# Packing the last 64 channels of two rows into one transpose in a fused dynamic-convolution and gated-FFN kernel

## The chip, the cores and the metric

The kernel runs on one core of a Trainium2 chip. The metric is the device time of one execution in microseconds (us), given as the median of three runs, with the lowest and highest beside it. The profile is one further execution of the same program, recorded by the hardware profiler; its span is counted from the first to the last instruction.

## The reference

Two stages in float32. First a dynamic convolution: for each of 4 x 4160 positions and 8 heads, seven softmax weights mix the current row of `x` (192 channels, 24 to a head) with the six rows before it. Then a gated feed-forward layer of width 1024, with a convolution of three taps over the positions inside the gate.

```python
w = exp(weight_gen - max); w = w / (sum(w) + 1e-9)          # [B, S, 8, 7]
y[b, s, h, :] = sum over k of w[b, s, h, k] * x_pad[b, s + k, h, :]
h = maximum(y @ w_in, 0)                                    # [B, S, 1024]
conv[s] = sum over k in 0..2 of conv_w[k] * h_pad[s + k]
out = (h * sigmoid(conv)) @ w_out                           # [B, S, 192]
```

## The kernel before, in words

The 16640 positions are dealt out as 130 consecutive rows to each of 128 partitions. They are worked through in 33 blocks `q` of R = 4 rows (512 positions).

**Taps and folds.** For each block, seven products of a row window with a weight (`tap`, L292) are written by GpSimd (POOL) or VectorE (DVE) into two tiles: `px` with four slots of 128 x (4 rows x 192 channels), and `py` with three. In blocks 0 to 2 TensorE (PE) adds the seven products itself, while it transposes them, in PSUM. In the other 30 blocks the sum is made before that: an accumulating DMA adds `py` onto `px[0:3]` (`fold1`, L315), a second one adds `px[2:4]` onto `px[0:2]` (`fold2`, L318), and one POOL addition of 768 elements per partition adds slot 1 onto slot 0 (`fold3`, L322). `px` has three buffers; taps of a later block wait until the transposes have read the old one.

**Transposes.** The folded block has positions on its partitions and must have channels there. `transposes` (L327) does this on PE in two parts through one PSUM bank, `tp`. Part 0 takes channels 0 to 127 of each of the four rows: four transposes, each with a loaded operand of 128 columns. Part 1 takes channels 128 to 191: four transposes with a loaded operand of 64 columns. Every transpose streams the 128 columns of an identity. After each part the PSUM bank is read by two engines: ScalarE (ACT) copies it into a rounded high part (`split_hi`, L338), then DVE subtracts that from the bank and writes the low part (`split_lo`, L343). Part 1 gives the tile `H2`, with the high part in partitions 0 to 63 and the low part in 64 to 127. Part 1 may overwrite the bank only after the subtraction of part 0.

**Feed-forward.** For each of eight groups `f` of 128 hidden channels, `mm1` (L359) runs five matmuls of 512 columns into one of five PSUM banks `z`; then follow `relu` and `wmid` on ACT, two side taps on DVE (L376), a tanh on ACT (L383) and the gate product on DVE (L392), which frees the bank. Two blocks later `mm2` (L405) runs four output tiles of eight accumulating matmuls, each of 192 columns.

**Order.** Every instruction is a task with an engine and an assumed duration. A planner, at the end of the function, places all tasks from those durations, once forward, once backward and once forward again, and the instructions are issued in the order of the planned starts. Each engine then runs its own list in that order and waits on semaphores.

Of the kernel before, what the change touches and what calls it, by code (L numbers as in the profile page):

```python
# [8 lines left out]
F32 = mybir.dt.float32  # L9
# [3 lines left out]
ACTF = mybir.ActivationFunctionType  # L13
ALU = mybir.AluOpType
AX = mybir.AxisListType

P = 128
# [34 lines left out]
def vec(n, ps=1):  # L52

    return 0.07 + n / 960 + 0.06 * ps


def act(n, ptr=0):
    return 0.05 + n / 1200 + 0.1 * ptr


def pool(n, ins=2):
    return (0.13 + n / 437) if ins == 2 else (0.1 + n / 900)
# [3 lines left out]
def kernel(  # L66
# [9 lines left out]
    nc = tc.nc  # L76
    B, S, D = x.shape
# [5 lines left out]
    D2 = D - P  # L83
# [7 lines left out]
    R = 4  # L91
# [18 lines left out]
    ident = const.tile([P, P], F32, name="ident")  # L110
# [73 lines left out]
    def group(q):  # L184
        return (q + 1) // 2
# [95 lines left out]
    def tap_cut(q, k):  # L281
        return max(0, slot(R * q - TAPS + k) + R - RING) % R
# [17 lines left out]
    px_t, py_t, h_t = {}, {}, {}  # L300

    def piece(q, i):
        if i < 4:
            if q not in px_t:
                px_t[q] = px_p.tile([P, 4, R, D], F32, tag="px", name="px")
            return px_t[q][:, i]
        if q not in py_t:
            py_t[q] = py_p.tile([P, 3, R, D], F32, tag="py", name="py")
        return py_t[q][:, i - 4]
# [4 lines left out]
    def fold1(q):  # L314
        nc.gpsimd.dma_start(out=fl4(px_t[q][:, 0:3]), in_=fl4(py_t[q][:, 0:3]), accum_op=ALU.add, max_dma_last_dim=3072)  # L315

    def fold2(q):
        nc.gpsimd.dma_start(out=fl4(px_t[q][:, 0:2]), in_=fl4(px_t[q][:, 2:4]), accum_op=ALU.add, max_dma_last_dim=3072)  # L318

    def fold3(q):  # L320
        a, b = (px_t[q][:, i].rearrange("p s d -> p (s d)") for i in range(2))
        nc.gpsimd.tensor_tensor(out=a, in0=a, in1=b, op=ALU.add)  # L322

    def transposes(q, i, part, dst, start, stop):
        src = piece(q, i)
        for c in range(R):
            nc.tensor.matmul(  # L327
                dst[0:D2 if part else P, c * P:(c + 1) * P],
                lhsT=src[:, c, part * P:part * D2 + P],
                rhs=ident, is_transpose=True, start=(start and c == 0), stop=(stop and c == R - 1),  # L330
            )

    def split_hi(q, part, tp):
        if (q, "H1") not in h_t:
            for nm in ("H1", "L1", "H2"):
                h_t[q, nm] = t_p.tile([P, W], F32R, tag=nm, name=nm)
        r = slice(0, D2 if part else P)
        nc.scalar.activation(out=h_t[q, "H2" if part else "H1"][r, :], in_=tp[r, :], func=ACTF.Copy)  # L338

    def split_lo(q, part, tp):  # L340
        H = h_t[q, "H2" if part else "H1"]
        r = slice(0, D2 if part else P)
        nc.vector.tensor_tensor(  # L343
            out=H[D2:P, :] if part else h_t[q, "L1"], in0=tp[r, :], in1=H[r, :].bitcast(F32), op=ALU.subtract
        )

    z_t, g_t = {}, {}

# [73 lines left out]
    V, G = nc.vector, nc.gpsimd  # L422

    with tc.manual_schedule():
# [7 lines left out]
        def load_in(eng, kind, a, b):  # L432
# [17 lines left out]
            out=ident, in_=ident, pattern=[[-1, P]], base=0, channel_multiplier=1,  # L450
# [4 lines left out]
            out=edge, in_=edge, pattern=[[1, TAPS], [1, TAPS]], base=-TAPS, channel_multiplier=0,  # L455
# [31 lines left out]
        def task(eng, dur, deps, fn=None, after=(), begun=()):  # L487
            edges = [(d, dur_of(d) + lat(d, eng)) for d in deps if d is not None]
            edges += [(d, dur_of(d)) for d in after if d is not None]
            edges += [(d, 0.0) for d in begun if d is not None]  # L490
            tasks.append((eng, dur, edges, fn))
            prio.append(now[0])
            return len(tasks) - 1

        def dur_of(d):
            return tasks[d][1]

        ENDS = {"V": 0.125, "A": 0.14, "G": 0.08, "P": 0.2, "D": 0.0, "H": 0.0, "none": 0.05}

        def lat(d, eng):  # L500
            e = tasks[d][0]
            if e == eng == "P":
                return 0.02
            return ENDS[e[0] if e != "none" else e] + {"P": 0.02, "G": 0.045}.get(eng, 0.0)

        def dma(occ, deps, fn):
            return task("none", 3.2, [task("H", occ, deps, fn)])

# [73 lines left out]
        for c, (kind, a, b, t, eng, wle) in enumerate(CH):  # L582
# [7 lines left out]
            if kind == "m":  # L590
                hi, lo = wh[:, 0, a:b], wl[:, 0, a:b]
            else:
                th = tB.bitcast(F32R).rearrange("p (l f) -> p l f", l=2)
                hi, lo = th[:, 0, 0:n], th[:, 1, 0:n]
            a_ = task("A", act(n) + 0.02, [j_], lambda bits=bits, hi=hi: nc.scalar.activation(  # L595
                out=hi, in_=bits().bitcast(F32), func=ACTF.Copy))
            if pm:
                wle = "V"
            b_ = task("V" if pm else "VK" if wle == "V" else "G", vec(n, pm) if wle == "V" else pool(n), [a_],
                      lambda bits=bits, hi=hi, lo=lo, wle=wle: (V if wle == "V" else G).tensor_tensor(  # L600
                out=lo, in0=bits().bitcast(F32), in1=hi.bitcast(F32), op=ALU.subtract))
# [7 lines left out]
            else:  # L609
# [10 lines left out]
                b_ = dma(2.6, [b_], spread)  # L620
# [19 lines left out]
        bank = {0: [c2], 1: [], 2: dbank[0]}  # L640
        NU = NB * NF

        def dadd(deps, occ, fn, e):
            return task("none", 3.2, [task("D", occ, [task("G", e, deps, fn)])])
# [9 lines left out]
        def head(q):  # L654
            how, engs = PLAN[q] if q < len(PLAN) else REST
            prod = {}
            xdep, ydep = xf_[-NX:][:1] if q >= NX else [], yf_[-NY:][:1] if q >= NY else []
            for i, k in ((0, 0), (1, 1), (2, 2), (4, 4), (5, 5), (6, 6), (3, 3)):
                e = engs[i]
                E_, d_ = (V, vec(R * D, 0)) if e == "V" else (G, 1.5)  # L660
                d_ += 0.14 * (tap_cut(q, k) > 0)
                p_ = task("VK" if e == "V" else e, d_, [sm[group(q)], x_t_[q]] + (xdep if i < 4 else ydep),
                          lambda E_=E_, k=k, i=i: tap(E_, q, k, piece(q, i)), begun=[gp[0]] if e == "G" else [])
                if e == "G":
                    gp[0] = p_
                prod[i] = p_
                all_taps.setdefault(q, []).append(p_)
            if how == "a":
                out_ = [(i, prod[i]) for i in (0, 1, 2, 4, 5, 6, 3)]
            else:  # L670
                a_ = dadd([prod[i] for i in (0, 1, 2, 4, 5, 6)], 6.5, lambda: fold1(q), 0.82)
                yf_.append(a_)
                out_ = [(3, prod[3]), (0, a_), (1, a_), (2, a_)]
                if how != "b":
                    a_ = dadd([a_, prod[3]], 4.4, lambda: fold2(q), 0.775)
                    out_ = [(0, a_), (1, a_)]
                    if how != "c":
                        out_ = [(0, task("G", 1.78, [a_], lambda: fold3(q)))]
            multi = len(out_) > 1
            now[0] = q + FO  # L680
            hold, prev = {}, [None, None]
            hd = [mm_end[q - 2]] if q >= 2 else []
            xend, yend = [], []
            for n, (i, e_) in enumerate(out_):
                first, last = n == 0, n == len(out_) - 1
                for part in (0, 1):
                    b_ = part if multi else 0

                    def fold(i=i, part=part, b_=b_, first=first, last=last):
                        if first:  # L690
                            hold[part] = (ps_o if b_ else ps_t).tile(
                                [P, W], F32, tag="ops" if b_ else "tp", name="ops" if b_ else "tp")
                        transposes(q, i, part, hold[part], first, last)
                    f_ = task("P", 0.46, [e_] + (bank[b_] if first else [prev[part]]), fold)
                    prev[part] = f_
                    (xend if i < 4 else yend).append(f_)
                    if last:
                        a_ = task("A", 0.49, [f_] + hd, lambda part=part: split_hi(q, part, hold[part]))
                        l_ = task("V", 0.6, [a_], lambda part=part: split_lo(q, part, hold[part]))
                        spl_done.setdefault(q, []).append(l_)  # L700
                        bank[b_] = [l_]
            xf_.append(task("none", 0.0, xend))
            if yend:
                yf_.append(task("none", 0.0, yend))
# [54 lines left out]
        def attention(q):  # L759
            now[0] = q + TO  # L760
            loads(q)
            head(q)
# [145 lines left out]
```

## Time and profile before

| | |
|---|---|
| median of 3 runs | 713.72 us (713.22 to 714.27) |
| the profiled execution's own time | 713.11 us |
| its span | 711.4 us |
| PE busy in the span | 690.1 us, 97% |
| PE weight loads (PEld) | 629.0 us, 88% |
| DVE busy | 625.6 us, 88% |
| ACT busy | 549.9 us, 77% |
| POOL busy | 510.5 us, 72% |

Busy shares are averages over the whole span, and matmuls overlap in the pipeline, so the length of one matmul's record is more than the time by which it delays the next. The chain that ended last follows the work back from the final instruction and gives each step only the time by which it delayed the end. In the page's 40 slices the granted clock of PE is at its top level (the digit 9, 2.4 GHz) throughout.

### The profile page before, as it was taken

The page shows a single profiled execution, that of the slowest core. Times are in us where ns is not written, and L with a number is a line of the kernel's source. Part 1 is how long each engine was busy: PE and PEld are TensorE (multiplying, and loading weights), DVE is VectorE, ACT ScalarE, POOL GpSimd, SP SyncE. Part 2 cuts the span into 40 slices and gives each one's busy share as a digit, 9 for nine tenths or more (in the row PEclk, how much of TensorE's full clock was granted, in tenths as well). Part 3 has the DMA queues.
Part 4 walks back from the last instruction along what each step waited for, and adds up shares of the span by engine and source line. Part 5 has one row for each costly group of instructions (what it writes and reads, how often), then busy time and mean ns, then how long its engine had stood idle before and what let it go on. Part 6 is the DMA issues. An engine that isn't in the chain of part 4 may idle for free.

```text
span 711.4 us, 10938 instructions
## 1 busy us (share of the span) xinstructions
PE 690.1 (97%) x3809; PEld 629.0 (88%) x3809; DVE 625.6 (88%) x975; ACT 549.9 (77%) x1049; POOL 510.5 (72%) x392
## 2 busy tenths in 40 slices
PE   1899999999999999999999999999999999999998
PEld 1788999999999999999999999999999999999998
DVE  6999998989999998998898988988898888888981
ACT  2588888887888787878787877878778778787881
POOL 3998999999987778887777778877767788630000
PEclk9999999999999999999999999999999999999999
DMA  7736999898989688798888788788879886781211
GB/s 226 212 98 166 215 217 225 211 236 197 229 186 211 166 208 200 167 209 189 193 193 200 190 181 202 184 200 193 188 181 200 178 183 163 163 181 68 76 43 45
DMA packets 70787, 127.59 MB, mean 179 GB/s; under 512 B 5046, under 2 KB 42573, under 8 KB 70732
## 3 DMA queue, kind: packets, MB, share of 16 engines
q0 software_dynamic: 20160, 58.99, 46.9%
q1 hardware_dynamic: 50090, 67.51, 29.3%
q8 instruction: 30, 0.49, 0.3%
q10 hardware_dynamic: 482, 0.40, 0.2%
q14 instruction: 25, 0.20, 0.1%
HBM read 20.51 MB, written 12.78 MB: 47 GB/s over the span
## 4 chain that ended last, share of the span: by engine, by line
PE 96%; DMA 2%; DVE 1%; POOL 0%; SPq 0%; ACT 0%; issue 0%; POOLq 0%
PE ops L405 47%; PE z L359 43%; PE tp L327 5%; DMA ring<-in_x_dram 1%; PE ops L327 1%; PE z L405 1%; DMA stage<-in_moe_w_in_dram 1%; DVE py L292 0%; POOL px L292 0%; POOL py L292 0%; SPq L437 0%; DVE r L257 0%; DVE m L248 0%; DVE w L242 0%; DVE px L292 0%
## 5 line engine op out<-in xcount | busy, mean ns | idle before, releaser
L376 DVE SCALAR_TENSOR_TENSOR z<-h,cw,z 128x512 f32<-128x512 f32 (+1 forms) x528 | 379.3, 741 | 25.7 <-ACT z L369 21.3
L405 PE MATMUL ops<-wo,g 128*128 128x192 f32 x2048 | 353.1, 326 | 0.0
L405 PEld LDWEIGHTS ops<-wo,g 128*128 128x128 f32 x2048 | 338.9, 190 | 10.0
L359 PE MATMUL z<-H,wi 128*128 128x512 f32 x1056 | 303.6, 409 | 1.0 <-ACT wi L595 1.0
L292 POOL TENSOR_TENSOR px<-ring,w 128x768 f32<-128x768 f32 (+2 forms) x146 | 231.9, 1702 | 79.6 <-PE tp L327 75.3
L359 PEld LDWEIGHTS z<-H,wi 128*128 128x128 f32 x1056 | 191.1, 189 | 32.5 <-ACT wi L595 1.4
L392 DVE SCALAR_TENSOR_TENSOR g<-z,h 128x512 f32<-128x512 f32 (+1 forms) x264 | 178.3, 679 | 22.3 <-ACT z L383 14.6
L383 ACT ACTIVATE z<-z 128x512 f32<-128x512 f32 (+1 forms) x264 | 151.3, 573 | 45.2 <-DVE z L376 43.4
L369 ACT ACTIVATE z<-h,cw 128x512 f32<-128x512 f32 (+1 forms) x264 | 179.9, 682 | 5.7
L365 ACT ACTIVATE h<-z 128x512 f32<-128x512 f32 x264 | 155.7, 590 | 29.1 <-PE z L359 27.8
L292 POOL TENSOR_TENSOR py<-ring,w 128x768 f32<-128x768 f32 (+2 forms) x108 | 162.8, 1813 | 2.2 <-DMA px<-py 2.2
L359 PE MATMUL z<-L,wi 128*128 128x512 f32 x264 | 103.1, 391 | 0.0
L322 POOL TENSOR_TENSOR px<-px 128x768 f32<-128x768 f32 x30 | 68.0, 2265 | 6.1 <-DMA px<-px 6.1
L414 ACT ACTIVATE o<-ops 128x192 f32<-128x192 f32 x128 | 41.9, 328 | 24.0 <-PE ops L405 22.8
L359 PEld LDWEIGHTS z<-L,wi 128*128 128x128 f32 x264 | 49.6, 188 | 11.2
L338 ACT ACTIVATE H<-tp 128x512 fp32r<-128x512 f32 (+1 forms) x63 | 37.3, 593 | 21.5 <-PE tp L327 20.1
L327 PE MATMUL tp<-ident,px 128*128 128x128 f32 (+1 forms) x288 | 44.5, 279 | 2.7 <-POOL px L292 1.9
L315 POOL DMA_DIRECT2D px<-py x30 | 41.3, 1377 | 7.2 <-POOL py L292 7.2
L318 POOL DMA_DIRECT2D px<-px x30 | 36.3, 1211 | 13.2 <-DMA px<-py 12.0
L327 PEld LDWEIGHTS tp<-ident,px 128*128 128x128 f32 (+1 forms) x288 | 34.6, 132 | 9.5 <-POOL px L292 2.4
L343 DVE TENSOR_TENSOR L<-tp,H 128x512 fp32r<-128x512 f32 x33 | 22.7, 687 | 6.9 <-ACT H L338 6.9
L343 DVE TENSOR_TENSOR H<-tp,H 64x512 fp32r<-64x512 f32 x30 | 20.5, 684 | 6.7 <-ACT H L338 5.9
(67 smaller groups left out, 180.4 us busy)
## 6 DMA issues: line engine op xcount, KB each, us to landing
px<-py POOLq DMA_DIRECT2D x30, 1152.0 KB, 10.2
h<-h SPq DMA_DIRECT2D x128, 256.0 KB, 4.4
px<-px POOLq DMA_DIRECT2D x30, 768.0 KB, 6.6
ring<-in_x_dram SPq DMA_DIRECT2D x31, 384.0 KB, 6.0
out_dram<-o SPq DMA_DIRECT2D x31, 384.0 KB, 2.4
w<-in_weight_gen_dram SPq DMA_DIRECT2D x15, 224.0 KB, 6.5
r_out<-in_moe_w_out_dram SPq DMA_DIRECT2D x4, 384.0 KB, 5.6
wi<-scr SPq DMA_DIRECT2D x8, 128.0 KB, 5.2
```

The source lines that it names most:

```text
L292: eng.tensor_tensor(out=dst[:, a:b, :].rearrange("p s (h g) -> p s h g", g=GRP), in0=ring[:, p:p + n, :].rearrange("p s (h g) -> p s h g", ...
L322: nc.gpsimd.tensor_tensor(out=a, in0=a, in1=b, op=ALU.add)
L327: nc.tensor.matmul(dst[0:D2 if part else P, c * P:(c + 1) * P], lhsT=src[:, c, part * P:part * D2 + P], rhs=ident, is_transpose=True, star ...
L343: nc.vector.tensor_tensor(out=H[D2:P, :] if part else h_t[q, "L1"], in0=tp[r, :], in1=H[r, :].bitcast(F32), op=ALU.subtract)
L359: nc.tensor.matmul(out=z, lhsT=w[:, fs], rhs=h_t[j, nm], start=(i == 0), stop=(i == len(terms) - 1))
L365: nc.scalar.activation(out=hrow(f, 2, R), in_=z_t[j, f], func=ACTF.Relu)
L369: nc.scalar.activation(out=z_t[j, f][:, :no * P], in_=hrow(f, cc, no), func=ACTF.Copy, scale=cw[:, NF + f:NF + f + 1])
L376: nc.vector.scalar_tensor_tensor(out=z, in0=hrow(f, cc + d, no), scalar=cw[:, k * NF + f:k * NF + f + 1], in1=z, op0=ALU.mult, op1=ALU.add,)
L383: nc.scalar.activation(out=z, in_=z, func=ACTF.Tanh, scale=0.5)
L392: nc.vector.scalar_tensor_tensor(out=g_of(j, f), in0=z_t[j, f][:, :no * P], scalar=1.0, in1=hrow(f, cc, no), op0=ALU.add, op1=ALU.mult)
L405: nc.tensor.matmul(out=ps[:, 0:D], lhsT=g_of(j, f)[:, i * P:(i + 1) * P], rhs=wo[:, f, :], start=(f == 0), stop=(f == NF - 1),)
L414: nc.scalar.activation(out=o_t[j][:, i, :], in_=ps[:, 0:D], func=ACTF.Copy, scale=0.5)
```

## The change

`fold3` becomes two POOL instructions instead of one. Both read slots 0 and 1 of `px` and write slot 2 (instead of slot 0) in another layout: first the first 128 channels of the four rows, 4 x 128 elements, then the last 64 channels of the four rows side by side, 4 x 64 elements. So in part 1 two rows fill one loaded operand of 128 columns, and part 1 takes two transposes instead of four; their result lies in all 128 partitions of 256 columns of the bank. As one of the two rows comes out in partitions 64 to 127, the split of part 1 runs as two instructions of 64 x 256 on ACT and two on DVE, one for each row of the pair. The numbers of the planner's tasks are changed with it. Blocks 0 to 2 (`i >= 0`) are as before.

```diff
     def fold3(q):
-        a, b = (px_t[q][:, i].rearrange("p s d -> p (s d)") for i in range(2))
-        nc.gpsimd.tensor_tensor(out=a, in0=a, in1=b, op=ALU.add)
+        c = px_t[q][:, 2].rearrange("p s d -> p (s d)")
+        a, b = px_t[q][:, 0], px_t[q][:, 1]
+        for lo, hi, dst in ((0, P, c[:, 0:R * P]), (P, D, c[:, R * P:])):
+            nc.gpsimd.tensor_tensor(
+                out=dst.rearrange("p (s d) -> p s d", s=R), in0=a[:, :, lo:hi], in1=b[:, :, lo:hi], op=ALU.add
+            )
+    R2 = R // 2
     def transposes(q, i, part, dst, start, stop):
-        src = piece(q, i)
-        for c in range(R):
+        if i < 0:
+            src = px_t[q][:, 2].rearrange("p s d -> p (s d)")
+            ops = [(dst[:, c * P:(c + 1) * P], src[:, (part * R + c) * P:(part * R + c + 1) * P])
+                   for c in range(R2 if part else R)]
+        else:
+            src = piece(q, i)
+            ops = [(dst[0:D2 if part else P, c * P:(c + 1) * P], src[:, c, part * P:part * D2 + P]) for c in range(R)]
+        for c, (o, a) in enumerate(ops):
             nc.tensor.matmul(
...
+    def parts(q, part, tp, pairs):
+        H = h_t[q, "H2" if part else "H1"]
+        if not part:
+            return [(tp, H, h_t[q, "L1"])]
+        if not pairs:
+            return [(tp[0:D2], H[0:D2], H[D2:P])]
+        rows = H.rearrange("p (a b t) -> p a b t", a=R2, b=2)
+        return [(tp[b * D2:(b + 1) * D2, 0:R2 * P].rearrange("p (a t) -> p a t", a=R2), rows[0:D2, :, b], rows[D2:P, :, b])
+                for b in range(2)]
...
+        for src, hi, lo in parts(q, part, tp, pairs):
+            nc.scalar.activation(out=hi, in_=src, func=ACTF.Copy)
+    def split_lo(q, part, tp, pairs):
+        for src, hi, lo in parts(q, part, tp, pairs):
+            nc.vector.tensor_tensor(out=lo, in0=src, in1=hi.bitcast(F32), op=ALU.subtract)
...
-                        out_ = [(0, task("G", 1.78, [a_], lambda: fold3(q)))]
+                        out_ = [(-1, task("G", 2.02, [a_], lambda: fold3(q)))]
...
-                    f_ = task("P", 0.46, [e_] + (bank[b_] if first else [prev[part]]), fold)
+                    pr = i < 0 and part == 1
+                    f_ = task("P", 0.24 if pr else 0.46, [e_] + (bank[b_] if first else [prev[part]]), fold)
...
-                        a_ = task("A", 0.49, [f_] + hd, lambda part=part: split_hi(q, part, hold[part]))
-                        l_ = task("V", 0.6, [a_], lambda part=part: split_lo(q, part, hold[part]))
+                        a_ = task("A", 0.56 if pr else 0.49, [f_] + hd, lambda part=part, pr=pr: split_hi(q, part, hold[part], pr))
+                        l_ = task("V", 0.78 if pr else 0.6, [a_], lambda part=part, pr=pr: split_lo(q, part, hold[part], pr))
```

## Rows read from the trace of the kernel before

**Rows 1.** The page: busy time of each engine, then the chain by engine.
```profile
PE 690.1 (97%) x3809; PEld 629.0 (88%) x3809; DVE 625.6 (88%) x975; ACT 549.9 (77%) x1049; POOL 510.5 (72%) x392
...
PE 96%; DMA 2%; DVE 1%; POOL 0%; SPq 0%; ACT 0%; issue 0%; POOLq 0%
```

**Rows 2.** All waits of PE: who for whom, us in total, times, longest.
```profile
PE tp L567 <- DVE tok L874: 14.4, 1, 14.4
PE tp L327 <- POOL px L292: 1.9, 2, 1.3
PE z L359 <- ACT wi L595: 1.0, 1, 1.0
PE tp L327 <- DVE px L292: 0.8, 1, 0.8
```

**Rows 3.** Busy time by stretch: the stretch, its length, each engine, clock, DMA.
```profile
75.00:697.00 622.00, 622.00 (x3412) 568.96 (x3411) 559.26 (x837) 499.02 (x940) 452.27 (x337) 1.00 0.80 183
```

**Rows 4.** The chain that ended last, 300 to 345 us: start, us, what.
```profile
303.33 0.44 PE tp L327 x4
...
319.58 0.44 PE tp L327 x4
320.02 1.16 PE z L359 x5
```

**Rows 5.** Transposes by shape: count, us busy, mean ns of one, idle before.
```profile
L327 PE MATMUL tp<-ident,px 128*128 128x128 f32 x168 | 26.5, 284 | 2.7 <-POOL px L292 1.9 <-DVE px L292 0.8
...
L327 PEld LDWEIGHTS tp<-ident,px 128*128 128x128 f32 x168 | 21.4, 147 | 7.9 <-POOL px L292 2.4 <-DVE px L292 1.2 <-issue 0.3
...
L327 PE MATMUL tp<-ident,px 128*64 128x128 f32 x120 | 18.0, 273 | 0.0
...
L327 PEld LDWEIGHTS tp<-ident,px 128*64 128x64 f32 x120 | 13.2, 112 | 1.5
```

**Rows 6.** The same view: copies and subtractions from PSUM, 512 and 256 columns.
```profile
L343 DVE TENSOR_TENSOR H<-tp,H 64x512 fp32r<-64x512 f32 x30 | 20.5, 684 | 6.7 <-ACT H L338 5.9
...
L338 ACT ACTIVATE H<-tp 64x512 fp32r<-64x512 f32 x30 | 17.7, 590 | 1.3
...
L600 DVE TENSOR_TENSOR wi<-dps,wi 128x256 fp32r<-128x256 f32 x2 | 0.8, 424 | 0.0
...
L595 ACT ACTIVATE wi<-dps 128x256 fp32r<-128x256 f32 x2 | 0.8, 383 | 3.8 <-DVE dps L151 3.8
```

**Rows 7.** The same view: POOL, the last fold and taps of several sizes.
```profile
L292 POOL TENSOR_TENSOR px<-ring,w 128x768 f32<-128x768 f32 x116 | 204.5, 1850 | 67.1 <-PE tp L327 62.8 <-DMA px<-py 4.1
...
L322 POOL TENSOR_TENSOR px<-px 128x768 f32<-128x768 f32 x30 | 68.0, 2265 | 6.1 <-DMA px<-px 6.1
...
L292 POOL TENSOR_TENSOR px<-ring,w 128x384 f32<-128x384 f32 x10 | 9.3, 1031 | 12.5 <-PE tp L327 12.5
...
L292 POOL TENSOR_TENSOR px<-ring,w 128x192 f32<-128x192 f32 x10 | 8.4, 836 | 0.0
```

**Rows 8.** POOL's longest wait, columns as in Rows 2.
```profile
POOL px L292 <- PE tp L327: 75.3, 20, 5.6
```

**Rows 9.** Timeline of the first folded block, 75 to 86 us: start, us, instruction.
```profile
75.32 2.22 POOL L322 TENSOR_TENSOR px<-px 128x768 f32<-128x768 f32 x1
...
77.80 0.60 PE L327 MATMUL tp<-ident,px 128*128 128x128 f32 x4
...
83.41 0.68 DVE L343 TENSOR_TENSOR H<-tp,H 64x512 fp32r<-64x512 f32 x1
...
84.90 1.23 PE L359 MATMUL z<-H,wi 128*128 128x512 f32 x4
```

**Rows 10.** Timeline of a later block, 300 to 321 us.
```profile
304.42 0.68 DVE L343 TENSOR_TENSOR H<-tp,H 64x512 fp32r<-64x512 f32 x1 [0.21 <-ACT H L338]
...
307.22 1.22 PE L359 MATMUL z<-H,wi 128*128 128x512 f32 x4
```

**Rows 11.** Busy time in one block's length, early and late: PE, PEld, DVE, ACT, POOL.
```profile
75.00:95.45 20.45, 20.45 (x114) 18.76 (x113) 20.23 (x31) 16.81 (x32) 19.78 (x18) 1.00 1.01 233
...
500.00:520.45 20.45, 20.45 (x114) 18.69 (x113) 17.86 (x29) 16.23 (x31) 15.39 (x12) 1.00 0.84 189
```

More of the change, by code (lines that the diff above doesn't have):

```diff
@@ L320, in fold3, with split_hi @@
     def fold3(q):
-        a, b = (px_t[q][:, i].rearrange("p s d -> p (s d)") for i in range(2))
-        nc.gpsimd.tensor_tensor(out=a, in0=a, in1=b, op=ALU.add)
-    def transposes(q, i, part, dst, start, stop):
-        src = piece(q, i)
-        for c in range(R):
+        c = px_t[q][:, 2].rearrange("p s d -> p (s d)")
[5 more added lines that the diff above has]
+    R2 = R // 2
+    def transposes(q, i, part, dst, start, stop):
+        if i < 0:
[6 more added lines that the diff above has]
+        for c, (o, a) in enumerate(ops):
             nc.tensor.matmul(
-                dst[0:D2 if part else P, c * P:(c + 1) * P],
-                lhsT=src[:, c, part * P:part * D2 + P],
-                rhs=ident, is_transpose=True, start=(start and c == 0), stop=(stop and c == R - 1),
-            )
-    def split_hi(q, part, tp):
+                o, lhsT=a, rhs=ident, is_transpose=True, start=(start and c == 0), stop=(stop and c == len(ops) - 1)
+            )
+    def parts(q, part, tp, pairs):
[7 more added lines that the diff above has]
+                for b in range(2)]
+    def split_hi(q, part, tp, pairs):
         if (q, "H1") not in h_t:
@@ L336, in split_hi @@
                 h_t[q, nm] = t_p.tile([P, W], F32R, tag=nm, name=nm)
[L337 to L345, printed above, removed]
+        for src, hi, lo in parts(q, part, tp, pairs):
[3 more added lines that the diff above has]
+            nc.vector.tensor_tensor(out=lo, in0=src, in1=hi.bitcast(F32), op=ALU.subtract)
     z_t, g_t = {}, {}
```

## The prediction

> **What bounds the kernel now.** I read the chain that ended last first, and in the page it sits beside the busy shares [rows 1]. The reader is to see two things. PE holds 96% of the chain, so time taken out of PE's list comes out of the end unless another engine is late in its place. And DVE is at 88% over the span, so it is the only engine near enough to become that other. The second view is PE's own waits [rows 2]: four lines, 18.1 us together, and no line in which PE waits for a fold after the first blocks, for the split of a block, or for the gate product that frees a `z` bank. The third view shows where these waits are: from 75 us, when the first fold of this kind runs, to 697 us, PE is busy for 622.00 of 622.00 us [rows 3]. All 30 folded blocks lie in that stretch. So each PE instruction removed there shortens the run by its pace, as long as the other lists keep up.
>
> **Step 1, the transposes.** The pace of a transpose is read from the chain, not from its record. The records last 273 ns [rows 5], but they overlap; in the chain four of them delay what follows by 0.44 us [rows 4], so 0.11 us each. The two rows of that 0.44 us are one group of part 1 (loaded operand of 64 columns, at 303.33) and one of part 0 (128 columns, at 319.58). They are equal, so the pace follows the 128 columns of the identity that stream through, which the change keeps, and not the width of the loaded operand, which it doubles. Part 1 runs in 30 blocks with four transposes each, which are the 120 matmuls of the 128*64 form [rows 5]; 60 remain. Gain: 60 x 0.11 = 6.6 us.
>
> Bounds. The new pair loads 128 columns right behind matmuls of another kind. A load of 128 columns is recorded at 147 ns and one of 64 at 112 ns [rows 5]; if the 35 ns of both loads were in the open, 30 x 2 x 0.035 = 2.1 us of the gain would go. In the other direction the matmuls behind a group of transposes take 1.16 us for five [rows 4] and stay as they are, so I see no gain beyond the 6.6 us here: the term lies between 4.5 and 6.6 us, and I take 6.6, since the part 0 group already has this load width and shows none of the 35 ns.
>
> The Trainium skill ("TensorE: Matmul & The Clock Gate", section "LDWEIGHTS (loading the stationary operand)") says that a load's time goes with the number of its columns, which would make one load of 128 as long as two of 64. By that rule, were loads the pace, the two wide transposes would cost as much as the four narrow ones and the sum would be no change; the rows have 147 against 112 ns, so here it is not double.
>
> **Step 2, POOL.** One addition of 768 elements, 2265 ns, becomes one of 512 and one of 256. Taps of 192, 384 and 768 elements take 836, 1031 and 1850 ns [rows 7]. On straight lines between them 512 elements cost 1.30 us and 256 cost 0.90 us, 2.20 us against 1.85 us; scaled by 2265/1850 the fold grows by up to 0.43 us. With the later, steeper line carried down to 256 the pair costs 2.06 us and the growth is 0.26 us. Either way it is hidden: POOL waits 75.3 us in all until PE has read an old `px` [rows 8], so it is ahead of PE, and in a late block it is busy for 15.39 of 20.45 us [rows 11]. The one place where the cover is thin is the first fold: it ends at 75.32 + 2.22 = 77.54 us and the transposes of part 0 start at 77.80 [rows 9]. Those need only the first of the two additions, which ends earlier than the single one does now. Should they wait for both, the loss is at most 0.43 - 0.26 = 0.2 us, once. The write to slot 2 adds no wait that the fold doesn't have: it reads slots 0 and 1, which the DMA that reads slot 2 must have finished. I take 0, with 0.2 us as the other end.
>
> **Step 3, the split of part 1.** ACT: 2 x 383 - 590 = 176 ns more for each block; DVE: 2 x 424 - 684 = 164 ns more [rows 6]. Queued behind the split on DVE are the side taps and gate products of the block before, and behind these, through the banks, PE's `mm1`. Two questions follow.
>
> First, does the first `mm1` of the block wait? The subtraction ends at 83.41 + 0.68 = 84.09 us in the first folded block, 0.8 us ahead of the `mm1` record at 84.90 [rows 9], and 2.1 us ahead in a later block (304.42 + 0.68 = 305.10 against 307.22) [rows 10]. The chain from the last transpose to the last subtraction grows by at most 0.18 + 0.16 = 0.34 us. The shorter group of transposes starts it 0.22 us earlier, but takes the same 0.22 us off the distance to `mm1` if nothing else lies between. So 0.34 us comes out of a cover of 0.8 us or more: cost 0. If a block had no cover at all, it would lose 0.34 us there, more than the 0.22 us it gained.
>
> Second, does DVE as a whole keep up? A late block has 17.86 us of DVE work in 20.45 us; 18.02 us then stands against a PE block of 20.23 us. An early block has 20.23 us [rows 11], and 20.39 us would be 0.16 us over the new PE block. That block also carries softmax steps of later blocks and gives the excess to the `z` banks, so I take 0; at the other end the two blocks in this state (75 to 116 us) would lose their 0.22 us and 0.16 us each, 0.8 us.
>
> **Step 4, the order.** The planner gets other durations for the fold, the transposes and the split, so the lists of all engines are placed anew, SP's with the carry, load and store DMAs and POOL's with the fold DMAs included. Number and size of all DMAs stay. What another order can do to PE is bounded by what it waits for now: of the 18.1 us, 14.4 us are before its first matmul, and 3.7 us are in the start [rows 2]. Another order can save that or double it, so plus or minus 3.7 us; nothing in the rows gives a sign, and I take 0.
>
> **Sum.** 713.11 us is the profiled execution's own time; less 6.6 us it is 706.5 us, a span of 704.8 us. The median shown is 0.61 us higher, and the forecast for a median is 713.72 - 6.6 = 707.1 us, 0.9% faster.
>
> **Rivals.**
>
> No gain, because loads set the pace. If each transpose took as long as its load, four of 112 ns are 0.448 us, which is also what the part 1 group takes. With the 147 ns of a wide load the pair would take 0.294 us and the gain would be 30 x 0.154 = 4.6 us, 709.1 us; with a wide load as long as two narrow ones, 0.448 us and no gain, 713.7 us. The part 0 group speaks against it: four loads of 147 ns would be 0.588 us, and it takes 0.44 us [rows 4, 5].
>
> Slower, because DVE becomes the bound. Place: DVE's list, which is worked in order, between the split and the gate products that free `z` banks. It decides from the point at which DVE's work in a block, idle stretches that it cannot use included, reaches PE's 20.23 us. Then PE's gain is worth nothing and each of 30 blocks grows by the 164 ns of the second subtraction: 713.7 + 4.9 = 718.6 us. For it speaks the early block, which is over that line by 0.16 us [rows 11]; against it, the late one with 2.2 us to spare and a PE without one wait for DVE after the start [rows 2, 3].
>
> A worse order. PE's waits of the start come twice, 3.7 us, and the gain is 2.9 us: 710.8 us. The mechanism is step 4; for it speaks only that all orders change, against it that PE is without a gap over 622 us under durations that the planner merely assumes.
>
> That the change does something other than it says shows in the count: 60 fewer transposes and 60 fewer loads.
>
> **How the numbers follow.** Forecast 0.79, with a range of its own from 705.8 to 709.2 us (the 2.1 us of open loads above it, a third of the start's 3.7 us below it). The worse order 0.10. Loads as the pace with no gain 0.05. DVE as the bound 0.06. A measurement of this kernel can tell a difference of 0.2%, 1.4 us, from none. Faster by more than that holds the forecast and the worse order, 0.89; within it is 0.05; slower 0.06. The range takes in the forecast's and most of the worse order: 705.4 to 710.8 us.
>
> **What would show it.** Step 1: the group of two in the chain takes 0.22 us, and a steady block 20.23 instead of 20.45 us. Step 2: two additions of together 2.5 to 2.7 us, and POOL still waiting tens of us for PE. Step 3: two copies near 383 ns and two subtractions near 424 ns per block, with no line in PE's waits for them. Step 4: PE's waits near 18 us in all. The prediction is wrong if PE, between the first fold and the last `mm1`, has waits that add up to more than a microsecond or two, or if the pair takes well over 0.22 us.

## The result and the profile after

| | before | changed |
|---|---|---|
| median in this comparison | 714.32 us (713.22 to 718.08) | 706.97 us (705.86 to 708.09) |
| the profiled execution's own time | 713.11 us | 706.31 us |
| its span | 711.4 us | 704.3 us |
| PE busy | 690.1 us | 683.6 us |

The ratio is 0.989, with a 95% interval from 0.9866 to 0.9915. The forecast was 707.1 us, worked out from a median of 713.72 us for the kernel before; its median in this comparison is 0.6 us higher.

The page of the changed kernel, busy times and chain by engine, answers to [rows 1]:
```profile
PE 683.6 (97%) x3749; PEld 623.3 (89%) x3749; DVE 629.0 (89%) x1005; ACT 554.5 (79%) x1079; POOL 514.9 (73%) x422
...
PE 96%; DVE 2%; DMA 1%; POOL 0%; issue 0%; ACT 0%; POOLq 0%
```
PE has 60 matmuls and 60 loads fewer and 6.5 us less of busy time; DVE has 3.4 us more, ACT 4.6 us and POOL 4.4 us. The chain is PE's as before.

All waits of PE in the changed kernel (who for whom, total us, times, longest), against [rows 2]:
```profile
PE tp L586 <- DVE tok L894: 13.8, 1, 13.8
PE tp L340 <- POOL px L292: 2.0, 2, 1.3
PE z L378 <- ACT wi L614: 1.0, 1, 1.0
PE tp L340 <- DVE px L292: 0.8, 1, 0.8
```
The same four, and none took the place of the work removed. Only the wait before the first matmul (the first line) is 0.6 us shorter. Over the profiles of all kernels in this document it lies between 13.8 and 15.1 us, so these 0.6 us can't be put down to the change.

The stretch from the first fold to the last blocks (its length, then busy us of PE, PEld, DVE, ACT, POOL), against [rows 3]:
```profile
75.00:690.00 615.00, 615.00 (x3349) 562.79 (x3348) 562.20 (x867) 503.03 (x970) 456.14 (x367) 1.00 0.81 184
```
PE is again without a gap, at the full clock of 2.4 GHz.

The chain from 300 to 345 us (start, us, what), against [rows 4]:
```profile
300.38 0.22 PE tp L340 x2
300.60 1.16 PE z L378 x5
...
316.43 0.44 PE tp L340 x4
...
320.62 0.22 PE tp L340 x2
```
Two wide transposes take 0.22 us where four narrow ones took 0.44, and the five matmuls behind them still take 1.16. A block, from one pair to the next, is 20.24 us long (300.38 to 320.62); it was 20.45, from the group at 303.33 to the next one of part 1 in the kernel before:
```profile
323.78 0.44 PE tp L327 x4
```
So of the 7.1 us that left the span, 30 x 0.22 = 6.6 us are step 1, and 0.6 us are the wait before the first matmul; together 7.2, with rounding.

The instructions that were split, by shape (us busy, mean ns of one, idle before), against [rows 5 to 7]:
```profile
L325 POOL TENSOR_TENSOR px<-px 128x512 f32<-128x512 f32 x30 | 52.3, 1745 | 5.3 <-DMA px<-px 5.3
...
L325 POOL TENSOR_TENSOR px<-px 128x256 f32<-128x256 f32 x30 | 35.6, 1188 | 0.0
L340 PEld LDWEIGHTS tp<-ident,px 128*128 128x128 f32 x228 | 30.0, 145 | 8.7 <-POOL px L292 2.5 <-DVE px L292 1.2 <-issue 0.3
L364 DVE TENSOR_TENSOR H<-tp,H 64x256 fp32r<-64x256 f32 x60 | 25.4, 423 | 7.7 <-ACT H L360 5.8
...
L360 ACT ACTIVATE H<-tp 64x256 fp32r<-64x256 f32 x60 | 22.6, 377 | 0.4
```
The copies and subtractions cost what the nearest rows said (377 for 383 ns, 423 for 424). The two additions have records of 1745 and 1188 ns, but they overlap: in the timeline of the changed kernel the pair lasts 2.45 us.
```profile
312.32 2.45 POOL L325 TENSOR_TENSOR px<-px 128x512 f32<-128x512 f32 x2
```

POOL's longest wait, against [rows 8]:
```profile
POOL px L292 <- PE tp L340: 67.0, 19, 4.9
```
It is 8.3 us shorter, and still long: POOL is ahead of PE.

A later block of the changed kernel (start, us, instruction), against [rows 10]:
```profile
300.64 0.76 ACT L360 ACTIVATE H<-tp 64x256 fp32r<-64x256 f32 x2
...
301.44 0.86 DVE L364 TENSOR_TENSOR H<-tp,H 64x256 fp32r<-64x256 f32 x2 [0.36 <-ACT H L360]
...
304.06 1.23 PE L378 MATMUL z<-H,wi 128*128 128x512 f32 x4
```
The two subtractions take 0.86 us and end at 302.30, 1.8 us ahead of the first `mm1` of the block; before it was 2.1 us.

### The profile page after: what moved, and what is told of

It reads as the page before. It is cut to its first block, busy times and chain, and to the rows that moved or that the text cites. A ratio compares the mean times of both kernels' runs of the same rounds, so it can differ in the third digit from the quotient of the medians.

```text
span 704.3 us, 10972 instructions
## 1 busy us (share of the span) xinstructions
PE 683.6 (97%) x3749; PEld 623.3 (89%) x3749; DVE 629.0 (89%) x1005; ACT 554.5 (79%) x1079; POOL 514.9 (73%) x422
## 4 chain that ended last, share of the span: by engine, by line
PE 96%; DVE 2%; DMA 1%; POOL 0%; issue 0%; ACT 0%; POOLq 0%
PE ops L424 47%; PE z L378 43%; PE tp L340 4%; PE ops L340 1%; DMA stage<-in_moe_conv_w_dram 1%; PE z L424 1%; DMA stage<-in_moe_w_in_dram 0%; DVE py L292 0%; POOL px L292 0%; POOL py L292 0%; DVE r L257 0%; DVE m L248 0%; DVE w L242 0%; DVE px L292 0%; DVE dps L146 0%
## 5 line engine op out<-in xcount | busy, mean ns | idle before, releaser
L325 POOL TENSOR_TENSOR px<-px 128x512 f32<-128x512 f32 (+1 forms) x60 | 72.9, 1466 | 5.3 <-DMA px<-px 5.3
L360 ACT ACTIVATE H<-tp 64x256 fp32r<-64x256 f32 (+1 forms) x93 | 42.3, 454 | 22.0 <-PE tp L340 21.7
L378 PEld LDWEIGHTS z<-L,wi 128*128 128x128 f32 x264 | 49.5, 188 | 11.2
L340 PE MATMUL tp<-ident,px 128*128 128x128 f32 x228 | 38.0, 281 | 2.8 <-POOL px L292 2.0
L340 PEld LDWEIGHTS tp<-ident,px 128*128 128x128 f32 x228 | 30.0, 145 | 8.7 <-POOL px L292 2.5
L364 DVE TENSOR_TENSOR H<-tp,H 64x256 fp32r<-64x256 f32 x60 | 25.4, 423 | 7.7 <-ACT H L360 5.8
```

The source lines that it names most:

```text
L325: nc.gpsimd.tensor_tensor(out=dst.rearrange("p (s d) -> p s d", s=R), in0=a[:, :, lo:hi], in1=b[:, :, lo:hi], op=ALU.add)
L340: nc.tensor.matmul(o, lhsT=a, rhs=ident, is_transpose=True, start=(start and c == 0), stop=(stop and c == len(ops) - 1))
L360: nc.scalar.activation(out=hi, in_=src, func=ACTF.Copy)
L364: nc.vector.tensor_tensor(out=lo, in0=src, in1=hi.bitcast(F32), op=ALU.subtract)
L378: nc.tensor.matmul(out=z, lhsT=w[:, fs], rhs=h_t[j, nm], start=(i == 0), stop=(i == len(terms) - 1))
```

## The experiments

The theory: the 60 transposes, at PE's pace, are the gain, and everything that the change adds is hidden. The rivals: the new order of the other engines carries part of it; loads set the pace; DVE is or becomes the bound. The change alters four durations of the planner, so the order is a part of it that can be taken alone: PE's list is the same in the kernels of the first four experiments but for the transposes themselves, while the lists of DVE, ACT, POOL and SP (SyncE, which issues DMAs) stand either in the order of before or in that of the changed kernel.

**First: all of the change in the order of before.**
```diff
-task("G", 2.02, ...)  task("P", 0.24 if pr else 0.46, ...)  task("A", 0.56 if pr else 0.49, ...)  task("V", 0.78 if pr else 0.6, ...)
+task("G", 1.78, ...)  task("P", 0.46, ...)  task("A", 0.49, ...)  task("V", 0.6, ...)
```


> All of the change, but the planner keeps the durations of before, so the instructions of every engine stand in the order of before. If the 60 transposes carry the gain (theory), a steady block is 20.24 us and the time is 706.5 to 708 us, within 1 us of the changed kernel. If the new order of ACT, DVE, POOL and SP carries part of it (rival), the time lies 2 us or more above the changed kernel, 709 us or more.

Measured: 709.13 us (707.65 to 710.1), ratio to before 0.9933 (0.9916 to 0.995). The rival's expectation held, though only just, and the theory's did not: the interval begins where that of the changed kernel ends (0.9866 to 0.9915). Its waits of PE have a line that neither the kernel before nor the changed one has:
```profile
PE tp L586 <- DVE tok L894: 14.8, 1, 14.8
PE tp L340 <- DVE L L364: 2.6, 1, 2.6
```
Part 1's transposes wait once, 2.6 us, until DVE has subtracted part 0 and so freed the bank. The timeline of that place shows why DVE was late:
```profile
154.17 0.97 POOL L242 TENSOR_TENSOR w<-w,m 128x448 f32<-128x448 f32 x1
...
155.18 0.58 ACT L245 ACTIVATE w<-w 128x448 f32<-128x448 f32 x1 [4.65 <-POOL w L242]
...
157.00 1.55 DVE L395 SCALAR_TENSOR_TENSOR z<-h,cw,z 128x512 f32<-128x512 f32 x2 [4.80 <-ACT z L388]
...
159.28 0.60 ACT L360 ACTIVATE H<-tp 128x512 fp32r<-128x512 f32 x1
...
161.50 0.68 DVE L364 TENSOR_TENSOR L<-tp,H 128x512 fp32r<-128x512 f32 x1
...
162.32 0.41 PE L340 MATMUL tp<-ident,px 128*128 128x128 f32 x2 [2.62 <-DVE L L364]
```
To be read downwards: an exp of the softmax of a later block stands in ACT's list and waits 4.65 us for POOL's subtraction. ACT works in order, so `wmid` and the copy of part 0 stand behind it; DVE idles 4.80 us for `wmid`, and works off what has piled up before it comes to part 0. In the kernel before, the same exp waited 1.55 us and nothing of it reached PE:
```profile
152.21 0.58 ACT L245 ACTIVATE w<-w 128x448 f32<-128x448 f32 x1 [1.55 <-POOL w L242]
```
In the changed kernel POOL's subtraction stands ahead of the fold's additions, and the exp finds it done:
```profile
146.40 1.45 POOL L242 TENSOR_TENSOR w<-w,m 128x448 f32<-128x448 f32 x1
...
148.83 0.58 ACT L245 ACTIVATE w<-w 128x448 f32<-128x448 f32 x1
```
The span here (708.2 us) is 3.9 us longer than that of the changed kernel. Of these, 2.6 us are this wait and 1.0 us the wait before the first matmul, which differs between kernels anyway; the profiled execution, 710.1 us, is also the longest of the six. The medians differ by 2.2 us.

**Second: the order of the changed kernel, with the code of before.** The four durations of the diff above in the kernel before.

> The code of before with the planner's durations of the changed kernel: its order of ACT, DVE, POOL and SP, but four narrow transposes, one fold, one split. Theory: a steady block stays at 20.45 us and the time at 713 to 714.5 us (at most the 0.6 us of a shorter wait before the first matmul is gained). Rival (the order): 2 us or more faster than before.

Measured: 713.99 us (712.52 to 715.07), ratio 1.0004 (0.9994 to 1.0015). The order by itself gains nothing where PE had no wait to lose.

**Third: each wide transpose twice.**
```diff
+            if part:
+                ops += [(dst[:, (R2 + c) * P:(R2 + c + 1) * P], src[:, (R + c) * P:(R + c + 1) * P])
+                        for c in range(R2)]
```


> The changed kernel, with each of the two wide transposes of part 1 issued a second time into the unused half of the bank (nothing reads that half). Four matmuls as before, but each with a load of 128 columns. If the count of transposes sets the cost (theory), the group takes 0.44 us in the chain and the time is 707.0 + 6.6 = 713.6 us. If the loads set it (rival), the group takes 4 x 0.147 = 0.59 us, 0.29 us more than two loads, 707.0 + 8.8 = 715.8 us.

Measured: 713.82 us (713.01 to 715.13), ratio 1.0001 (0.999 to 1.0012). The chain:
```profile
303.67 0.44 PE tp L343 x4
304.11 1.17 PE z L381 x5
```
Four loads of 128 columns, and 0.44 us as with four of 64. The number of transposes sets the time, not the width of what they load; two more for each of 30 blocks take back all that the change gained. The Trainium skill ("TensorE: Matmul & The Clock Gate", section "LDWEIGHTS (loading the stationary operand)") has the time of a load grow with its columns. The records agree in direction, 147 ns for 128 columns against 112 for 64 [rows 5]; the chain does not follow them.

**Fourth: only the split of part 1 in two, in the order of before.**
```diff
+        n = 2 if part and q >= len(PLAN) else 1
+        for b in range(n):
+            c = slice(b * W // n, (b + 1) * W // n)
             ...
```


> The kernel before, with only the split of part 1 in the folded blocks cut into two instructions of 64 x 256 on ACT and on DVE, in the order of before. Theory: DVE gets 164 ns more per block, 4.9 us in all, and PE doesn't see it: no change, 713 to 715 us. Rival (DVE sets the pace): 4.9 us slower, 718.6 us, with waits of PE for DVE.

Measured: 715.13 us (714.59 to 718.32), ratio 1.0022 (1.001 to 1.0033): slower, by about a quarter of what the rival asked, and the theory's "no change" fails as well. PE's waits name the place of the first experiment again:
```profile
PE tp L327 <- DVE L L349: 1.5, 1, 1.5
```
The exp there waited 3.99 us for POOL:
```profile
154.35 0.97 POOL L242 TENSOR_TENSOR w<-w,m 128x448 f32<-128x448 f32 x1
...
155.36 0.58 ACT L245 ACTIVATE w<-w 128x448 f32<-128x448 f32 x1 [3.99 <-POOL w L242]
```

**Fifth: the first again, with the exp later in ACT's list.** This tells apart whether ACT's list or DVE's time is at fault.
```diff
             for i, (e, d, fn) in enumerate(sm_ops(q)):
+                if i == 2 and q >= WB:
+                    t_ = task("none", 3.0, [t_])
```


> The first experiment again (all of the change, durations of before), with one thing more: the planner is told that the softmax subtraction on POOL has 3 us more of latency, so the exp that reads it stands later in ACT's list. The first experiment lost 2.6 us in one wait of PE on the subtraction of part 0, behind an ACT that had stood 4.65 us at an exp. Theory (ACT's list is held by the exp that waits for POOL): that wait of PE is gone and the time is 706.3 to 707.7 us. Rival (DVE has too little time for its second subtraction): the wait stays, 709 us.

Measured: 707.48 us (706.52 to 708.5), ratio 0.9908 (0.9887 to 0.9928). The line of 2.6 us is gone:
```profile
PE tp L588 <- DVE tok L896: 14.0, 1, 14.0
PE tp L340 <- POOL px L292: 1.3, 1, 1.3
PE z L378 <- ACT wi L616: 1.0, 1, 1.0
PE tp L340 <- DVE px L292: 0.8, 1, 0.8
```
The exp now waits for nothing:
```profile
156.30 0.58 ACT L245 ACTIVATE w<-w 128x448 f32<-128x448 f32 x1
```
DVE has the same instructions as in the first experiment, so its total was not at fault; the order was. The edit moves more than the exp, because the planner places all tasks anew: the softmax's reduction on DVE (L248, 0.61 us), for one, ran just ahead of the subtraction of part 0 in the first experiment and runs behind it here. That alone is less than the 2.6 us. How much the exp's own place is worth was not run by itself. The intervals of the two ratios overlap a little (0.9916 to 0.995 in the first), so it is the line of 2.6 us, there and gone, that carries this; the tenth experiment shows it with times that don't overlap.

**Sixth: only the fold in two additions.** Slot 2 as the target, four narrow transposes, one split, order of before.
```diff
-        nc.gpsimd.tensor_tensor(out=a, in0=a, in1=b, op=ALU.add)
+        for lo, hi, dst in ((0, P, c[:, 0:R * P]), (P, D, c[:, R * P:])):
             ...
+                lhsT=src[:, o + c * w:o + (c + 1) * w] if new else src[:, c, part * P:part * D2 + P],
```


> The kernel before, in its order, with only the fold in two POOL additions into slot 2; four narrow transposes and one split as before. If POOL's longer fold makes it late for the exp (theory), ACT waits about 4 us for POOL once near 155 us, PE waits 1 to 2.6 us there, and the time is 1 to 2 us above before, 715 to 716 us. If POOL's own waiting for px hides the fold everywhere, as the prediction had it (rival), there is no wait of PE after 75 us and the time is 713.9 us.

Measured: 713.91 us (712.28 to 716.45), ratio 0.9993 (0.9979 to 1.0008). My expectation here was wrong: the longer fold does not make POOL late for the exp (it waited 1.38 us, against 1.55 in the kernel before), and PE has no wait after 75 us. Step 2 of the prediction stands.

**Seventh and eighth: more DVE work.** The subtraction of part 0 issued twice, and four times, in each folded block of the changed kernel.
```diff
-        for src, hi, lo in parts(q, part, tp, pairs):
+        for src, hi, lo in parts(q, part, tp, pairs) * (2 if not part and q >= len(PLAN) else 1):   # 4 in the eighth
             nc.vector.tensor_tensor(out=lo, in0=src, in1=hi.bitcast(F32), op=ALU.subtract)
```


> The changed kernel with the subtraction of part 0 issued twice in each folded block (the second writes the same values): 0.6 to 0.69 us more DVE work per block, 18 to 20 us in all. If DVE isn't the bound (theory), at most the early blocks show it: 707 to 709 us. If DVE sets the pace already (rival), 707 + 18 = 725 us.

> The same with three more subtractions per block, 1.8 to 2.07 us. Theory: a late block then has 17.9 + 2 = 19.9 us of DVE work against PE's 20.24 and still holds, an early one with softmax has 19.1 to 19.6 + 2 = 21.4 and doesn't: about 1.2 us in each of some 15 blocks, 717 to 730 us, with PE waits for DVE in the first half and few in the second. Rival (DVE sets the pace everywhere): 707 + 54 to 62 = 761 us or more.

Measured: 707.67 us (707.0 to 708.58) and 733.3 us (732.89 to 734.21); ratios to before 0.9911 (0.9887 to 0.9935) and 1.0267 (1.0239 to 1.0295). One more subtraction, 30 of 0.69 us or some 20 us of DVE work, moves the median by 0.7 us, within the spread of the changed kernel's own runs. Three more move it by 26.3 us, more than I expected. Busy time with three more (length, then PE, PEld, DVE, ACT, POOL), an early and a late stretch, its chain by engine, and PE's longest wait:
```profile
75.00:115.50 40.50, 37.99 (x206) 34.07 (x205) 39.33 (x61) 30.08 (x61) 37.11 (x32) 1.00 0.92 204
...
500.00:581.00 81.00, 78.25 (x424) 70.80 (x423) 75.45 (x119) 61.42 (x120) 60.68 (x51) 1.00 0.80 178
```
```profile
DVE 73%; issue 10%; ACT 10%; PE 5%; DMA 1%; POOL 0%; DVEq 0%; POOLq 0%
```
```profile
PE tp L340 <- DVE L L364: 21.1, 28, 1.8
```
In the early stretch DVE is at 97% and PE loses 2.5 of 40.5 us. In the late one DVE still has 5.5 us to spare in 81, and PE loses 2.75 us all the same: the extra subtractions lie between part 0 and the release of the bank, and part 1 waits for that 28 times. So in the late stretch it is the length of that one chain that gives way and not DVE's total; I had only counted the total. In the early stretch the two can't be told apart, and over the whole run the chain that ended last is DVE's for 73%.

**Ninth: a version meant to be faster,** with block 2 folded once by DMA.
```diff
 PLAN = (
     ("a", "GVGGVGG"),
     ("a", "GGGGGGG"),
-    ("a", "GGGGGGG"),
+    ("b", "GGGGGGG"),
```


> The changed kernel, with block 2 folded once by the first accumulating DMA, so that PE transposes four pieces of it instead of seven: 24 transposes fewer before 75 us, 24 x 0.11 = 2.6 us. If PE's count decides there too, 704.4 us. DVE is busy for 47.2 of the 48 us from 27 to 75 us there and the fold's DMA needs some 10 us, so a wait may take the place of it (rival): 706 to 710 us. I expect the rival rather than the gain.

Measured: 714.88 us (713.8 to 716.8), ratio 1.0018 (1.0007 to 1.0028), 7.9 us above the changed kernel and outside both expectations. PE's waits:
```profile
PE tp L340 <- DVE L L364: 4.0, 1, 4.0
PE z L378 <- DVE g L411: 1.8, 2, 1.2
```
The start of the run (27 to 60 us), here and in the changed kernel:
```profile
27.00:60.00 33.00, 28.77 (x165) 23.07 (x164) 32.58 (x67) 28.15 (x58) 30.67 (x21) 1.00 0.65 178
```
```profile
27.00:60.00 33.00, 31.99 (x196) 27.09 (x195) 32.56 (x67) 28.57 (x59) 32.68 (x24) 1.00 0.49 147
```
PE is busy for 28.77 of 33 us there, where the changed kernel has 31.99: the 2.6 us of transposes are not saved but waited, beside a DVE that is busy for 32.58. That doesn't explain 7.9 us. The longest wait, 4.0 us, lies far behind block 2, and it is the place of the first experiment again, at another exp:
```profile
203.75 0.58 ACT L245 ACTIVATE w<-w 128x448 f32<-128x448 f32 x1 [6.69 <-POOL w L242]
204.24 0.58 ACT L360 ACTIVATE H<-tp 128x512 fp32r<-128x512 f32 x1
...
204.90 0.68 DVE L364 TENSOR_TENSOR L<-tp,H 128x512 fp32r<-128x512 f32 x1
...
205.73 0.66 PE L340 MATMUL tp<-ident,px 128*128 128x128 f32 x2 [4.02 <-DVE L L364]
```
PE pays for this gap twice. The granted clock falls from 1.00 to 0.50 (1.2 GHz) while PE stands idle and is still there at 210 us, so that the 16 matmuls of `mm2` in that time take 3.89 us and not 2.76 as elsewhere:
```profile
208.00:210.00 2.00, 2.00 (x8) 1.90 (x7) 1.84 (x5) 1.93 (x6) 1.74 (x3) 0.50 0.11 17
```
```profile
208.32 3.89 PE L424 MATMUL ops<-wo,g 128*128 128x192 f32 x16
```
So the edit shows two things at once, a start in which PE waits for what it saves and a new order with a hole in it, and does not show what the fold of block 2 is worth in a good order. No kernel run here is told to be faster than the changed one.

**Tenth and eleventh: the late exp with the split alone, and with the kernel before.** The edit of the fifth in the fourth, and in the kernel before.

> The fourth experiment again (before, with only the split of part 1 in two), with the exp placed later in ACT's list as in the fifth. The fourth was 1.3 us slower than before, with one wait of 1.5 us of PE on the subtraction of part 0. Theory (the split itself costs nothing, the list of ACT held at the exp does): the wait is gone and the time is 713.5 to 714.5 us. Rival (the 164 ns of DVE per block cost it): 715 us stay.

> The kernel before with only the exp placed later, as the control of the fifth and the tenth. PE has no wait there after the start in the profile of before, so nothing is to be gained: 713.5 to 714.5 us (theory). If the late exp frees time by itself (rival), 712.5 us or less.

Measured: 712.96 us (712.38 to 713.78), ratio 0.9988 (0.9979 to 0.9996), and 713.61 us (711.94 to 714.68), ratio 0.9992 (0.9983 to 1.0002). With the exp later the split costs nothing: no run of the tenth (712.38 to 713.78) reaches one of the fourth (714.59 to 718.32), and the wait of 1.5 us is gone from its profile. POOL's subtraction is as late as in the fourth, but the exp now comes after it:
```profile
154.83 0.98 POOL L242 TENSOR_TENSOR w<-w,m 128x448 f32<-128x448 f32 x1
...
157.47 0.59 ACT L245 ACTIVATE w<-w 128x448 f32<-128x448 f32 x1
```
So POOL being late does no harm here by itself; an ACT list that stands waiting for it does. The control is not told from before.

## Why the prediction was right

**Step 1** held in its size: 0.22 us for the pair, a block of 20.24 us where 20.23 was forecast, 6.6 us in all. The lower bound, 2.1 us of loads in the open, did not show: the matmuls behind the pair take 1.16 us as before. The third experiment shows that the pace is that of the count. That the 128 streamed columns set the 0.11 us, as the prediction argues, is not shown, as no run changed them. The rival of loads as the pace falls with it, and with it the reading by which the load's width would have eaten the gain.

**Step 2** held: the pair of additions lasts 2.45 us, less than the 2.5 to 2.7 forecast, and the fold alone changes nothing (sixth).

**Step 3** held in its sizes and in its sum, but I looked for the wait in the wrong place. I asked whether the first `mm1` waits for the split of part 1. The place that gives way first is one step earlier: part 1's transposes behind part 0's subtraction, through the one bank. The prediction names that dependency nowhere. It is covered in the changed kernel, and open by 2.6 us in the first experiment, by 1.5 us in the fourth, by 21.1 us in the eighth and by 4.0 us in the ninth.

**Step 4** held in its value for the changed kernel and not in its working. I bounded the effect of another order by PE's waits in the start and found no sign. The runs give one: with the order of before the same change takes 709.13 us instead of 706.97, 2.2 us more, and the profile has a wait of 2.6 us in one block, up to 162.3 us and not in the start. So the new durations given to the planner are worth about a third of the gain of the transposes. They do not speed anything up (second); with them ACT's list does not stand at an exp while the split waits behind it. That such a stand is what costs the time is shown by the first against the fifth and the fourth against the tenth. The prediction did not foresee that the new durations avoid it; that part is luck.

**The rivals.** DVE as the bound did not come: one more subtraction per block, four times what the change adds, costs 0.7 us. A worse order is the mechanism that came nearest: the same change in the order of before takes 709.13 us, which the stated range, up to 710.8 us, would have taken in as well.

**The number.** 706.97 us against a forecast of 707.1 us is closer than the working earned. The interval of the ratio leaves a gain between 6.1 and 9.6 us; the median before was 0.6 us higher here than the one used; and 0.6 us of the shorter span lie in the wait before the first matmul, which differs by more than that between kernels.

**What stays open.** Why POOL is 3 us later at that exp in the first and fourth experiments. Its list stands behind the landing of the first accumulating DMA there, for 2.78 and 2.45 us in two blocks of the first experiment where the kernel before has 1.24 and 1.26 us: for the folds issued between 100 and 156 us the median time to landing is 11.2 and 11.5 us in these two, 9.9 us in the kernel before and 10.7 us in the sixth. What delays the transfer was not tried by itself.

## What to carry to other kernels

If one engine is without a gap over the stretch in question, an instruction removed from its list was worth, here, its pace in the chain of waits, and neither its record nor its operand's width told it. What the change adds elsewhere is to be checked against the shortest cover, and that is a chain through one buffer and the in-order list of each engine on it: here a transpose behind a subtraction behind a copy behind an exp of another block. A planner's durations belong to the change; leaving them as they were would have cost about 2 us of its 7.

## What was not expected of the hardware

The records of two POOL additions in a row overlap: 1745 and 1188 ns last 2.45 us together, 0.48 us less than their sum, so that the pair costs less than the prediction's bounds from single records; two subtractions of 423 ns on DVE last 0.86 us and don't overlap. And the wait that decided 2 us of this case stood on an engine, ACT, that was busy for only 78% of the span in that run.
